# The top bits of the weights' low words: cut out by ScalarE from a byte, instead of by VectorE with a shift

## The chip, the cores and the metric

The kernel runs on one core of a Trainium2 chip. The metric is device time in microseconds (us) of one execution. TensorE multiplies matrices, VectorE and ScalarE work on tiles of 128 partitions, GpSimd does a few multiplications, and SyncE's queue (SP) issues nearly all DMAs. Each engine runs its own instructions in the order in which the program gives them, and waits on semaphores for the others.

## The reference

The queries, keys and values arrive as 32-bit floats, the weights as 64-bit floats. The computation is attention over 4 batches of 8 heads (576 positions, 64 wide), followed by two feed-forward layers on the 2304 x 512 result:

```
scores = q @ k^T / sqrt(64), masked: heads 0-3 a local window of 32,
         heads 4-7 every 32nd position (both causal)
x = softmax(scores) @ v                      # 2304 x 512
x = ((x @ w_a) * (x @ w_b)) @ w_out          # 512 -> 1536 -> 512
h = x @ w_in
out = (h * sigmoid(h)) @ w_out2              # 512 -> 2048 -> 512
```

## The kernel before

The 64-bit weights are read as pairs of 32-bit integers, low word first. The kernel puts each pair together to one 32-bit float with integer operations, and then splits that float into a rounded part and a remainder, with which each product takes three matmul passes.

The weights are cut into 68 pieces of 128 x 512: 36 for the first layer (kinds a, b and o) and 32 for the second (i and p). The work of the two layers is a list of 340 blocks; each block uses one piece on one group of up to 512 tokens and has 12 matmuls. The order of phases is: first layer of group 0, first layer of group 1, second layer of group 0, second layer of group 1, then the other groups. In the first round over the pieces a block also merges the piece that a later block needs: `conv_at` says that block p merges piece p + 3 up to block 32, and from block 34 on one piece in every 1.8 blocks. Six pieces (`EARLY`) are merged still earlier, during the attention of batch 0, with `early=True`. The attention of the other three batches is spread over the blocks as background work.

A merge has these steps, each an instruction on a 128 x 512 tile:

- `rebase_w` (L570, ScalarE): scales the high word as a float into the tile e.
- `merge_w` step 0 (L582, VectorE): takes the top three bits of the low word into a new tile "raw".
- step 1 (L585, VectorE): takes the sign bit of the high word and joins it to "raw".
- step 2 (L590, VectorE): shifts e left by three and joins "raw" to it. Now raw holds the float.
- `keep_w` (L601, SP): writes raw to DRAM, from where later groups load it again (`load_raw`, L560).
- `split_w` (L608 on ScalarE, L609 on VectorE): rounded part and remainder of a piece, into the tile w that the matmuls read.

In a block the order of the steps is given by a string of letters, 0, 1, 2 for the merge steps, B for the rebase, K for keep, Y for split, O for the attention output, X for its softmax, W for loads:

```
STEPS = ("RM0BK1O2YXWN", "0O1B2MKWYRXN")
```

The first string holds for blocks 0 to 35, the second for the others. Ahead of these steps the block puts its matmuls into TensorE's queue, with the background's loads, matmuls and copies of turned probabilities (L461, L467) before them; behind the steps it puts the evacuation of its PSUM tile: a copy (L818) for kind a, a product (L821) and a split (L626, L627) for kind b, a tanh (L825), a product (L827) and a split for kind i. So an engine meets the steps of block p only after the evacuation of block p-1.

The tiles "raw" come from a pool of five buffers, which merged pieces share with pieces that are loaded again; the words from another of five, the tiles e from one of two. A new tile waits until the readers of the former tile in its buffer, DMAs among them, are done.

The functions that the change touches:

Of the kernel before, what the change touches and what calls it, by code (L numbers as in the profile page):

```python
# [10 lines left out]
F32R = mybir.dt.float32r  # L11
BF16 = mybir.dt.bfloat16
I32 = mybir.dt.int32
AF = mybir.ActivationFunctionType
ALU = mybir.AluOpType
AX = mybir.AxisListType
# [71 lines left out]
def attention_gated_mlp_silu_mlp(  # L88
# [15 lines left out]
    nc = tc.nc  # L104
# [84 lines left out]
    class Batch:  # L189
# [213 lines left out]
        def softmax(self, u):  # L403
# [10 lines left out]
            for s in range(segs):  # L414
                nc.scalar.activation(  # L415
                    out=place[s],
                    in_=src[:, s],
                    func=AF.Exp,
                    bias=st["nm"][:, s:s + 1],
# [114 lines left out]
    words, raw, split, kept, rebased, loaded = {}, {}, {}, {}, {}, set()  # L534

    def load_words(c):
# [4 lines left out]
        w = {"a": w_a, "b": w_b, "o": w_out, "i": w_in2, "p": w_out2}[kind]  # L541
        words[c] = t = kpool.tile([P, 2 * DM], I32, tag="words", name="words")
        if kind in "op":
# [19 lines left out]
    def rebase_w(c, early=False):  # L563
# [4 lines left out]
        high = words[c].rearrange("p (n two) -> p n two", two=2)[:, :, 1]  # L568
        rebased[c] = e = epool.tile([P, DM], I32, tag="e", name="e")
        nc.scalar.activation(out=e.bitcast(F32), in_=high.bitcast(F32), func=AF.Copy, scale=REBASE)  # L570

    made = {}

    def merge_w(c, step, early=False):
        if c is None or (c < EARLY and not early):
            return
        pair = words[c].rearrange("p (n two) -> p n two", two=2)
        low, high = pair[:, :, 0], pair[:, :, 1]
        if step == 0:
            made[c] = rpool.tile([P, DM], F32, tag="raw", name="raw")  # L580
            z = made[c].bitcast(I32)
            nc.vector.tensor_single_scalar(out=z, in_=low, scalar=29, op=ALU.logical_shift_right)  # L582
        elif step == 1:
            z = made[c].bitcast(I32)
            nc.vector.scalar_tensor_tensor(  # L585
                out=z, in0=high, scalar=SIGN, in1=z, op0=ALU.bitwise_and, op1=ALU.bitwise_or
            )
        else:
            z = made[c].bitcast(I32)
            nc.vector.scalar_tensor_tensor(  # L590
                out=z, in0=rebased.pop(c), scalar=3, in1=z, op0=ALU.logical_shift_left, op1=ALU.bitwise_or
            )
            del words[c]
            if c < NA:
                raw[c] = made[c]
# [76 lines left out]
    def block(p):  # L672


        background(p, "load", "tensor", "turned")
        w = split.pop(p)
        yield w
        c = conv_at.get(p)
        for step in STEPS[p >= NA]:
            if step == "K":  # L680
                keep_w(conv_at.get(p - 1))
            elif step == "B":
                rebase_w(c)
            elif step in "012":
                merge_w(c, int(step))
            elif step == "Y":
                split_w(p + AHEAD_SPLIT)
                if p >= NB - NP:
                    split_w(p + AHEAD_SPLIT + 1)
            elif step == "W":  # L690
                load_words(conv_at.get(p + AHEAD_WORDS - AHEAD_MERGE))
                load_raw(p + (7 if p < last_conv + 2 else 9))
            else:
                background(p, {"M": "mask", "O": "store", "X": "softmax", "N": "normalise", "R": "prepare"}[step])
        yield None


    with tc.manual_schedule():
# [51 lines left out]
        for s in range(-1, max(nu + LV, max(PART), max(CONV) + 1) + 1):  # L750
# [7 lines left out]
            for step in ORDER:  # L758
# [4 lines left out]
                elif step in "SVTXLGNOU":  # L763
                    f, d = {
                        "S": (batch.scores, 0), "L": (batch.largest, 0), "X": (batch.softmax, 1),
                        "G": (batch.guard, 1), "N": (batch.normalise, 1), "T": (batch.turn, LT),
                        "U": (batch.turned, LT), "V": (batch.values, LV), "O": (batch.store, LV),
                    }[step]
                    stage(f, d)
                elif step == "K":  # L770
                    keep_warm(WARM1.get(s, 0))
                elif step == "A" and s in PART:
                    i = PART[s]
                    partial[i] = acc_tile(i)
                    up(partial[i], split[i], x_tile(0), G, (0, 1))
                elif step == "Q":
                    for i in TQ.get(s, ()):
                        batch.transpose_qk(1, i)
                elif step == "R":
                    for u in PREP.get(s, ()):  # L780
                        batch.prepare(u)
                elif step in "012" and now is not None:
                    merge_w(now, int(step), True)
                elif step == "B" and now is not None:
                    rebase_w(now, True)
                elif step == "Y" and last is not None and last < EARLY:
                    keep_w(last)
                    split_w(last)
                elif step == "W":
                    startup_loads(LOADS.get(s, ""))  # L790
        batch = after
        every(batch.load_vl())
        p = 0
        ys = {}
        for ph, g in PHASES:
# [7 lines left out]
            for kind, j in half[ph]:  # L803
# [4 lines left out]
                if kind in "abi":  # L808
# [14 lines left out]
                    else:  # L823
                        th = tpool.tile([P, G], F32, tag="a", name="th")
                        nc.scalar.activation(out=th[:, :T], in_=ps[:, :T], func=AF.Tanh, scale=0.5)  # L825
                        g2 = tpool.tile([P, G], F32, tag="h32", name="g2")
                        nc.vector.scalar_tensor_tensor(  # L827
                            out=g2[:, :T], in0=th[:, :T], scalar=1.0, in1=ps[:, :T], op0=ALU.add, op1=ALU.mult
                        )
                        hs[j] = split_act(g2, T)  # L830
                elif kind == "o":
# [10 lines left out]
                    if j == N1 - 1:  # L842
                        ys[g] = y = xpool.tile([P, 2, CC, G], F32R, tag="x%d" % HOMES["y"][g], name="y")
                        for d in range(CC):
                            nc.scalar.copy(out=y[:, 0, d, :T], in_=accs[d][:, :T])
                            nc.vector.tensor_tensor(
                                out=y[:, 1, d, :T],
                                in0=accs[d][:, :T],
                                in1=y[:, 0, d, :T].bitcast(F32),
                                op=ALU.subtract,  # L850
# [78 lines left out]
```

## Time and profile before

| | |
|---|---|
| time, median of 3 runs | 982.34 us (982.01 to 983.16) |
| profiled execution | 982.31 us |
| its span, first to last instruction | 980.5 us |
| mean granted TensorE clock | 0.993 of full speed |
| busy TensorE / VectorE / ScalarE / GpSimd | 958.2 / 611.4 / 474.5 / 40.3 us |

The span is the time from the first to the last instruction of the profiled execution; the time around it, 1.81 us, belongs to the device time. Durations below come from this execution. A busy engine isn't an engine at its peak: matmuls are pipelined and their ends are modelled, so that 12 matmuls that follow each other at their pace are listed with 2.88 us but start 2.72 us apart from the next twelve. In a timeline, a number in brackets is the time that the engine was idle just before the instruction, and the instruction that ended it.

### The profile page before, as it was taken

Reading aid. Unit: us, or ns where it says so; the run is one execution under the profiler, and the core shown is the slowest. Engines: PE = TensorE matmul, PEld = TensorE weight load, DVE = VectorE, ACT = ScalarE, POOL = GpSimd, SP = SyncE. Lnnn points to the kernel's source line nnn. Section 1 sums busy time; section 2 is a strip of 40 time slices with the busy share of each in tenths; the row PEclk is TensorE's granted clock in tenths of the full one; section 3 lists DMA queues with packets and bytes.
Section 4 is the critical chain, followed back from the end, with each engine's and each line's share of the span. In section 5 each row is a group of like instructions: output and inputs, shape, how many; then the busy total and the mean of one; then the engine's idle time right before and its main releaser. Section 6 shows DMA issues by size and latency. Waiting matters only on the chain.

```text
span 980.5 us, 16035 instructions
## 1 busy us (share of the span) xinstructions
PE 958.2 (98%) x5740; PEld 781.7 (80%) x5746; DVE 611.4 (62%) x1160; ACT 474.5 (48%) x1142; POOL 40.3 (4%) x66
## 2 busy tenths in 40 slices
PE   9989999999998999999999999999999999999998
PEld 5767677788777778888887888888888888889997
DVE  4788888878777864554644456554544454456675
ACT  3655556544555544544344445444333353445564
POOL 2100000000000000100000000000000000000000
PEclk9999999999999999999999999999999999999999
DMA  8899868898876763543364333323433323246551
GB/s 169 195 245 288 253 190 240 254 307 249 252 233 201 234 186 106 152 111 98 99 182 101 100 89 87 87 76 94 143 97 96 98 86 100 94 137 199 181 183 65
DMA packets 177647, 155.79 MB, mean 159 GB/s; under 512 B 102048, under 2 KB 125088, under 8 KB 177568
## 3 DMA queue, kind: packets, MB, share of 16 engines
q1 hardware_dynamic: 174198, 149.73, 53.2%
q0 software_dynamic: 1280, 4.20, 1.2%
q10 hardware_dynamic: 2090, 0.84, 0.4%
q8 instruction: 45, 0.74, 0.3%
q14 instruction: 34, 0.28, 0.1%
HBM read 132.19 MB, written 22.54 MB: 158 GB/s over the span
## 4 chain that ended last, share of the span: by engine, by line
PE 81%; DVE 9%; DMA 4%; issue 2%; ACT 2%; SPq 1%; DVEq 0%; ACTq 0%
PE ring L616 43%; PE acc L863 19%; PE acc L835 12%; PE att L378 2%; DVE raw L585 2%; DVE w L609 2%; PE att L489 1%; DVE raw L582 1%; DVE raw L590 1%; DMA vl<-in_v_dram 1%; DMA keptb<-raw 1%; DMA pair<-in_k_dram 1%; ACT h L626 1%; DMA kepta<-raw 1%; PE att L449 1%
## 5 line engine op out<-in xcount | busy, mean ns | idle before, releaser
L616 PE MATMUL ring<-x,w 128*128 128x512 f32 (+1 forms) x1392 | 303.0, 372 | 1.1 <-DVE w L609 1.1
L609 DVE TENSOR_TENSOR w<-raw,w 128x512 fp32r<-128x512 f32 x340 | 226.5, 685 | 87.3 <-ACT w L608 82.2
L616 PEld LDWEIGHTS ring<-x,w 128*128 128x128 f32 x1392 | 242.6, 190 | 46.3 <-DVE w L609 2.3
L616 PE MATMUL ring<-y,w 128*128 128x512 f32 (+1 forms) x960 | 211.4, 370 | 2.3 <-DVE w L609 2.2
L863 PE MATMUL acc<-w,h 128*128 128x512 f32 x864 | 212.1, 394 | 1.3 <-DVE w L609 1.3
L608 ACT CAST w<-raw 128x512 fp32r<-128x512 f32 x340 | 201.4, 618 | 10.0 <-DVE raw L590 9.6
L616 PEld LDWEIGHTS ring<-y,w 128*128 128x128 f32 x960 | 167.8, 188 | 34.3 <-DVE w L609 3.6
L863 PEld LDWEIGHTS acc<-w,h 128*128 128x128 f32 x864 | 160.5, 189 | 36.0 <-DVE w L609 2.2
L835 PE MATMUL acc<-h,w 128*128 128x512 f32 (+1 forms) x720 | 161.5, 374 | 0.3 <-DVE h L821 0.3
L835 PEld LDWEIGHTS acc<-h,w 128*128 128x128 f32 x720 | 126.0, 190 | 23.9 <-DVE h L821 0.7
L827 DVE SCALAR_TENSOR_TENSOR g<-th,ring 128x512 f32<-128x512 f32 (+1 forms) x80 | 50.5, 632 | 89.7 <-ACT th L825 88.5
L825 ACT ACTIVATE th<-ring 128x512 f32<-128x512 f32 (+1 forms) x80 | 44.3, 553 | 111.9 <-PE ring L616 111.6
L626 ACT CAST h<-h 128x512 fp32r<-128x512 f32 (+1 forms) x60 | 34.7, 578 | 121.4 <-DVE h L821 121.4
L627 DVE TENSOR_TENSOR h<-g,h 128x512 fp32r<-128x512 f32 (+1 forms) x80 | 51.1, 639 | 51.5 <-ACT h L626 51.5
L818 ACT COPY a<-ring 128x512 f32<-128x512 f32 (+1 forms) x58 | 31.4, 542 | 105.2 <-PE ring L616 105.2
L626 ACT CAST h<-g 128x512 fp32r<-128x512 f32 (+1 forms) x80 | 46.2, 578 | 70.1 <-DVE g L827 70.1
L627 DVE TENSOR_TENSOR h<-h,h 128x512 fp32r<-128x512 f32 (+1 forms) x60 | 38.3, 639 | 38.6 <-ACT h L626 38.6
L415 ACT ACTIVATE prs<-sm,nm 128x54 f32<-128x54 f32 (+1 forms) x120 | 39.8, 333 | 35.5 <-DVE nm L401 35.5
L440 POOL TENSOR_TENSOR prs<-prs,rs 128x256 f32<-128x256 f32 (+3 forms) x36 | 27.5, 764 | 587.6 <-ACT w L608 290.4
L590 DVE SCALAR_TENSOR_TENSOR raw<-e,raw 128x512 int32<-128x512 int32 x68 | 46.9, 689 | 6.3 <-ACT e L570 0.9
L821 DVE TENSOR_TENSOR h<-ring,a 128x512 f32<-128x512 f32 (+1 forms) x58 | 36.5, 629 | 22.1 <-PE ring L616 22.0
L585 DVE SCALAR_TENSOR_TENSOR raw<-words,raw 128x512 int32<-128x512 int32 x68 | 48.4, 712 | 2.3
(111 smaller groups left out, 513.3 us busy)
## 6 DMA issues: line engine op xcount, KB each, us to landing
raw<-kepti SPq DMA_DIRECT2D x80, 256.0 KB
raw<-keptp SPq DMA_DIRECT2D x80, 256.0 KB
words<-in_moe_w_out_dram SPq DMA_DIRECT2D x28, 512.0 KB
raw<-kepta SPq DMA_DIRECT2D x48, 256.0 KB
raw<-keptb SPq DMA_DIRECT2D x48, 256.0 KB
raw<-kepto SPq DMA_DIRECT2D x48, 256.0 KB
words<-in_moe_w_in_dram SPq DMA_DIRECT2D x16, 512.0 KB
words<-in_moe_w_a_dram SPq DMA_DIRECT2D x12, 512.0 KB
```

Source lines behind the costliest of these rows:

```text
L415: nc.scalar.activation(out=place[s], in_=src[:, s], func=AF.Exp, bias=st["nm"][:, s:s + 1], scale=1.0, accum_out=su[:, s:s + 1],)
L585: nc.vector.scalar_tensor_tensor(out=z, in0=high, scalar=SIGN, in1=z, op0=ALU.bitwise_and, op1=ALU.bitwise_or)
L590: nc.vector.scalar_tensor_tensor(out=z, in0=rebased.pop(c), scalar=3, in1=z, op0=ALU.logical_shift_left, op1=ALU.bitwise_or)
L608: nc.scalar.copy(out=o[:, 0], in_=t)
L609: nc.vector.tensor_tensor(out=o[:, 1], in0=t, in1=o[:, 0].bitcast(F32), op=ALU.subtract)
L616: nc.tensor.matmul(ps[:, :T], lhsT=w[:, wi, c * P:(c + 1) * P], rhs=x[:, xi, c, :T], start=(c == 0 and wi == 0 and xi == 0), stop=(c == CC ...
L626: nc.scalar.copy(out=o[:, 0, :T], in_=t32[:, :T])
L627: nc.vector.tensor_tensor(out=o[:, 1, :T], in0=t32[:, :T], in1=o[:, 0, :T].bitcast(F32), op=ALU.subtract)
L825: nc.scalar.activation(out=th[:, :T], in_=ps[:, :T], func=AF.Tanh, scale=0.5)
L827: nc.vector.scalar_tensor_tensor(out=g2[:, :T], in0=th[:, :T], scalar=1.0, in1=ps[:, :T], op0=ALU.add, op1=ALU.mult)
L835: nc.tensor.matmul(accs[d][:, :T], lhsT=w[:, wi, d * P:(d + 1) * P], rhs=h[:, xi, :T], start=(j == 0 and wi == 0 and xi == 0), stop=(j == ...
L863: nc.tensor.matmul(accs[t][:, :DM], lhsT=h[:, xi, t * P:(t + 1) * P], rhs=wj[:, wi, :], start=(jj == 0 and wi == 0 and xi == 0), stop=(jj ...
```

## The change

Step 0 of the merge, for all but the six early pieces, becomes an instruction of ScalarE. It reads the words as bytes, takes of each pair the fourth byte (the top byte of the low word), multiplies it by 1/32 and subtracts 31/64; written as the nearest integer, this is the byte divided by 32 and rounded down, which are the top three bits. Its place in the program is that of the instruction before: in ScalarE's queue it stands ahead of the rebase of the same piece.

```diff
+U8 = mybir.dt.uint8
 ...
         if step == 0:
             made[c] = rpool.tile([P, DM], F32, tag="raw", name="raw")
             z = made[c].bitcast(I32)
-            nc.vector.tensor_single_scalar(out=z, in_=low, scalar=29, op=ALU.logical_shift_right)
+            if early:
+                nc.vector.tensor_single_scalar(out=z, in_=low, scalar=29, op=ALU.logical_shift_right)
+            else:
+                top = words[c].bitcast(U8).rearrange("p (n eight) -> p n eight", eight=8)[:, :, 3]
+                nc.scalar.activation(out=z, in_=top, func=AF.Copy, scale=1.0 / 32, bias=-31.0 / 64)
```

## Rows read from the trace of the kernel before

**Rows 1.** Page: busy us of each engine; chain that ended last, by engine, by line

```profile
PE 958.2 (98%) x5740; PEld 781.7 (80%) x5746; DVE 611.4 (62%) x1160; ACT 474.5 (48%) x1142; POOL 40.3 (4%) x66
...
PE 81%; DVE 9%; DMA 4%; issue 2%; ACT 2%; SPq 1%; DVEq 0%; ACTq 0%
PE ring L616 43%; PE acc L863 19%; PE acc L835 12%; PE att L378 2%; DVE raw L585 2%; DVE w L609 2%; PE att L489 1%; DVE raw L582 1%; DVE raw L590 1%; DMA vl<-in_v_dram 1%; DMA keptb<-raw 1%; DMA pair<-in_k_dram 1%; ACT h L626 1%; DMA kepta<-raw 1%; PE att L449 1%
```

**Rows 2.** Stretches: length, busy us of each engine; clock, DMA share, GB/s

```profile
100.00:125.00 25.00, 21.32 (x119) 16.25 (x119) 22.09 (x49) 14.55 (x32) 0.40 (x1) 0.93 0.80 241
500.00:600.00 100.00, 100.00 (x599) 80.42 (x599) 49.46 (x94) 43.96 (x105) 3.69 (x5) 1.00 0.38 101
```

**Rows 3.** Waits of TensorE: line <- what it waited for, us in total, times, longest

```profile
PE att L489 <- ACT ptl L461: 5.8, 4, 2.7
PE ring L616 <- DVE w L609: 3.3, 4, 1.5
PE att L378 <- DVE x L512: 2.7, 2, 2.4
...
PE acc L863 <- DVE w L609: 1.3, 2, 0.8
```

**Rows 4.** Groups by line: tile shapes, count, busy us, mean ns, idle before

```profile
L608 ACT CAST w<-raw 128x512 fp32r<-128x512 f32 x340 | 201.4, 618 | 10.0 <-DVE raw L590 9.6
...
L585 DVE SCALAR_TENSOR_TENSOR raw<-words,raw 128x512 int32<-128x512 int32 x68 | 48.4, 712 | 2.3
...
L570 ACT ACTIVATE e<-words 128x512 f32<-128x512 f32 x68 | 45.9, 675 | 1.5 <-DMA words<-in_moe_w_b_dram 1.3
...
L582 DVE TENSOR_SCALAR raw<-words 128x512 int32<-128x512 int32 x68 | 29.1, 428 | 1.7 <-DMA keptb<-raw 1.6
```

**Rows 5.** Timeline of TensorE: start us, length us, instructions, idle before

```profile
101.50 0.69 PE L489 MATMUL att<-ptl,vl 128*64 128x64 f32 x16 [2.38 <-ACT ptl L461]
102.11 4.60 PE L616 MATMUL ring<-x,w 128*128 128x512 f32 x12
...
110.15 2.88 PE L835 MATMUL acc<-h,w 128*128 128x512 f32 x12
...
125.19 1.58 PE L378 MATMUL att<-kT,qs 64*64 64x54 f32 x18 [2.37 <-DVE x L512]
126.69 3.67 PE L616 MATMUL ring<-x,w 128*128 128x512 f32 x9
...
187.03 8.00 PE L616 MATMUL ring<-x,w 128*128 128x512 f32 x34 [0.86 <-DVE w L609]
...
292.04 2.59 PE L616 MATMUL ring<-y,w 128*128 128x512 f32 x10 [1.54 <-DVE w L609]
...
300.54 1.12 PE L489 MATMUL att<-ptl,vl 128*64 128x64 f32 x16 [2.68 <-ACT ptl L461]
...
324.05 2.56 PE L616 MATMUL ring<-y,w 128*128 128x512 f32 x10 [0.64 <-DVE w L609]
```

**Rows 6.** Timelines of VectorE (DVE) and ScalarE (ACT), 80 to 125 us

```profile
80.93 0.43 DVE L582 TENSOR_SCALAR raw<-words 128x512 int32<-128x512 int32 x1 [1.64 <-DMA keptb<-raw]
...
99.34 0.68 DVE L821 TENSOR_TENSOR h<-ring,a 128x512 f32<-128x512 f32 x1
...
102.01 0.39 DVE L582 TENSOR_SCALAR raw<-words 128x512 int32<-128x512 int32 x1
...
124.85 0.28 DVE L512 TENSOR_TENSOR x<-att,x 128x128 fp32r<-128x128 f32 x1
...
84.48 0.68 ACT L570 ACTIVATE e<-words 128x512 f32<-128x512 f32 x1 [1.32 <-DMA words<-in_moe_w_b_dram]
...
100.70 0.74 ACT L461 COPY ptl<-att 64x256 f32<-64x256 f32 x2
101.47 0.69 ACT L570 ACTIVATE e<-words 128x512 f32<-128x512 f32 x1
```

## The prediction, made before the kernel was run

> **What bounds the kernel now.** I read the page first: busy times, then the chain that ended last. TensorE is busy for 958.2 of 980.5 us and carries 81% of the chain, so most of the time is matmuls that the change doesn't touch; VectorE has 9% of the chain, and the three merge lines and the split (L582, L585, L590, L609) are its largest entries [rows 1]. The reader is to see that the share of L582 in the chain, 1%, is small but not nothing.
>
> An average hides where this is, so next come the stretches. From 100 to 125 us, where one weight piece is merged in each block, VectorE is busy 22.09 of 25 us, and what is left is mostly the pauses between dependent instructions; TensorE is busy for only 21.32. From 500 to 600 us, with no merge, TensorE is busy all of the time and VectorE half [rows 2]. ScalarE has 14.55 of 25 us in the first stretch. All L582 instructions lie before 351 us, so nothing after that can gain.
>
> Third, what TensorE waited for. Four rows name a late VectorE or ScalarE: 5.8, 3.3, 2.7 and 1.3 us, 13.1 together [rows 3]. This is the ceiling of a direct gain, plus what the clock adds: after the two long pauses of [rows 5] the next matmuls run slower (12 in 4.60 us, and 9 in 3.67, where 12 take 2.88), and the mean granted clock of that stretch is 0.93 against 1.00 later [rows 2, 5], so part of it ran at 1.2 instead of 2.4 GHz. That is some 1.7 and 1.5 us more (3.67 - 9/12 x 2.88 = 1.5).
>
> **The change part by part.** It removes 62 of the 68 L582 instructions from VectorE (the six early pieces keep theirs): 62 x 0.428 = 26.5 us of its time [rows 4]. It adds 62 ACTIVATEs to ScalarE. None in the trace reads bytes and writes integers. The nearest is L570, which reads one 32-bit word in every 8 bytes, as the new one reads one byte in every 8: 0.675 us; the cast L608, without a stride, takes 0.618; the far end would be the longest single-tile VectorE pass over such data, 0.712 [rows 4], and 1.0 if the byte input costs extra, which no row shows. I take 0.675, so 41.9 us more on ScalarE. No DMA, no matmul and no PSUM slot is added.
>
> What moves with it are the waits: for the loaded words and for a free "raw" buffer. They stand now in VectorE's queue and will stand in ScalarE's, ahead of the rebase, the attention output, the split and the softmax of the block. And L585 gets a wait it doesn't have now, for ScalarE; behind it on VectorE are L590, L609 and the next evacuation, for which TensorE waits in [rows 3].
>
> Does ScalarE come early enough? The new instruction stands directly ahead of the rebase L570, and L570 was idle for only 1.5 us over all its 68 instances [rows 4]: ScalarE walks straight into it, and stands still after it, where it needs VectorE. So the start of L570 is where the new one will start. In all ten blocks from 88 to 124 us L570 starts ahead of L582; the narrowest pair is 101.47 against 102.01 [rows 6]. The result is then ready at 101.47 + 0.675 + 0.05 for the semaphore = 102.2, where L585 without L582 could start at 102.0: a loss of 0.2 at the worst, none at most others. The saving per block on VectorE is thus the 0.43 of L582.
>
> *First place, 80 to 126 us.* Here VectorE runs almost without a gap, and both long TensorE pauses end on it: that at 101.50 through the probability copy (ptl) at 100.70, which ScalarE reaches only after a cast for which it waited on VectorE's L821 at 99.34; and that at 125.19 through the attention remainder (x) of 124.85 [rows 5, 6]. Twelve L582 lie between 80.9 and 124 us. Ten of them are met with VectorE late: 10 x 0.43 = 4.3. Two (the first is the 80.93 one, which had waited 1.64 for a DMA; the second comes at 84.49 with the words that L570 waited for until 84.48 [rows 6]) are released by DMA, and there the path becomes 0.675 + 0.05 instead of 0.43: 2 x 0.3 = 0.6 lost. The narrow pair costs 0.2, and the split behind it, which ScalarE reaches 0.57 later, about 0.1. So 4.3 - 0.6 - 0.3 = 3.4: TensorE restarts at 121.8 instead of 125.19. What the first pause gives back, its 1.7 us of low clock included, is swallowed by this second one. Whether the low clock after the second goes is unclear: 0 to 1.5, and I take 0, since the pause shrinks but the work around it is still small attention matmuls.
>
> *Second place, 150 to 250 us.* The rest of the L378 row (2.7 - 2.37 = 0.35) goes, since VectorE is then 3 us earlier. The 0.86 at 187.03 [rows 5] follows two L582 that stand between VectorE's last wait on TensorE and this split: 0.86, of which 0.2 is lost because the new instruction then stands behind the four y casts: 0.65. The two small waits in the L489 row (5.8 - 2.38 - 2.68 = 0.75) lie behind at least one L582 each: 0.75. Sum 1.75.
>
> *Third place, 285 to 355 us.* 1.54 at 292.04 and 2.68 at 300.54 come from one run of VectorE with two L582: 0.85 of the 4.22. The 0.64 at 324.05 lies behind two: it goes. The 1.3 of the L863 row [rows 3], at about 345 and 353, lies behind five: it goes. Sum 2.8.
>
> *Against it:* at 82.0 us an attention remainder frees a PSUM tile for TensorE's scores just in time; the DMA-released block ahead of it now has the new instruction in ScalarE's queue before the x cast: 0.4. Bounds of this term are 0 and 1.5.
>
> Sum: 3.4 + 1.75 + 2.8 - 0.4 = 7.55. The profiled execution took 982.31 (980.5 of span and 1.81 around it), 0.03 under the median of 982.34. So 982.31 - 7.5 = 974.8. If all terms are at their good ends (low clock gone, 0.43 everywhere, nothing against): 982.3 - 7.95 - 1.5 - 0.9 = 972; if freed time also lets the first place start earlier, down to 968, since 13.1 + 3.2 is all there is (966).
>
> **Rivals.**
> *A: the loads are the bound in the first place.* From 100 to 125 us the DMA engines are 0.80 busy [rows 2], and two of the twelve merges there were released by a DMA. If the words or the buffers' write-backs are late for all of them, VectorE only waits longer, and only the second and third places give: 982.3 - 4.5 + 0.6 = 978.4. Against it: ten of twelve didn't wait.
>
> *B: ScalarE becomes the bound and it gets slower.* Mechanism: the new instruction holds ScalarE's queue for a DMA or a buffer that VectorE's own order freed before; rebase, x cast, split and softmax stand behind it, and TensorE behind these. Place: the first, up to block 32. Price per block 0.675 + 0.05 - 0.43 = 0.3, and 30 merges lie there: 9 us; the later places then also give about 2 instead of 4.5: 982.3 + 9 - 2 = 989. It decides from where more than some fifteen of the thirty are released late (15 x 0.3 = 4.5, the gain of the others). For it: two such blocks are seen, and in block pairs without an evacuation ScalarE must now wait for VectorE's L609 to free a buffer. Against it: that lead in all ten blocks, of which [rows 6] shows the narrowest, and 10.4 us of spare ScalarE time in 25 [rows 2]. The Trainium skill ("ScalarE: Activation LUTs", Rules for kernel authors) speaks for this rival: it says that multiplies and adds belong on VectorE, not ScalarE. The rows agree on the price (0.675 against 0.428), not on which engine is late; by that rule the time would be this rival's.
>
> *C: no difference.* The gain in the first place is lost to A, and ScalarE's later splits cancel the rest (4.5 - 0.6 - 3): 981.4. Or the new instruction takes 1.0 us, which uses up the shorter leads.
>
> **How the numbers follow.** Forecast (970 to 977.5, named as 974.8): 0.58. A: 0.15. C: 0.12. B: 0.15. A measurement of this kernel can tell 0.2%, 2 us, from no change. Faster by over 0.2% is the forecast and A: 0.73; within it C: 0.12; slower B: 0.15. The range from 968 to 984 holds the forecast, A and C, and leaves out most of B and a gain beyond all named waits.
>
> **What would show it.** Right: VectorE some 26 us less busy, ScalarE some 42 more; the new line 0.62 to 0.71 us; the waits of TensorE at about 125, 187, 324 and 345 us gone or smaller, that at 300 still there; L585 with little idle time for the new line. Wrong: idle time of VectorE before L585 of more than 5 us, put down to ScalarE; ScalarE idle before the new line for DMA or L609; new TensorE waits on splits or x; or the same waits of TensorE with a DMA as their end.

## The result, and the profile after

The changed kernel took 976.81 us in the median of 9 runs (972.15 to 980.58), the kernel before in the same rounds 983.91 (982.01 to 989.81). The ratio is 0.991 with a 95% interval of 0.9883 to 0.9938: 6 to 11.5 us faster. The profiled execution took 977.48 us, with a span of 975.7.

Page after: busy us of each engine; the chain by engine and line (lines have moved: the new instruction is L589, the former L585, L590, L608, L609 are L592, L597, L615, L616).

```profile
PE 959.9 (98%) x5746; PEld 782.9 (80%) x5746; DVE 587.4 (60%) x1098; ACT 508.0 (52%) x1204; POOL 41.5 (4%) x66
...
PE 85%; DVE 7%; ACT 2%; DMA 2%; issue 2%; SPq 1%; DVEq 0%; ACTq 0%
```

Against [rows 1], VectorE is 24.0 us less busy and ScalarE 33.5 more (its 41.5 of new work, of which each instruction overlaps the next by some 0.1 us), and TensorE's share of the chain rose from 81% to 85%.

Groups by line after: shapes, count, busy us, mean ns, idle before:

```profile
L592 DVE SCALAR_TENSOR_TENSOR raw<-words,raw 128x512 int32<-128x512 int32 x68 | 47.3, 695 | 13.8 <-ACT raw L589 13.2
...
L571 ACT ACTIVATE e<-words 128x512 f32<-128x512 f32 x68 | 45.3, 667 | 0.0
L589 ACT ACTIVATE raw<-words 128x512 int32<-128x512 uint8 x62 | 41.5, 670 | 4.2 <-DMA keptb<-raw 2.3 <-DMA words<-in_moe_w_b_dram 1.1 <-DVE w L616 0.6
```

The new instruction takes 0.670 us, as the rebase beside it; the byte input and the integer output cost nothing extra. The waits for DMA that stood at L570 and L582 [rows 4] stand at L589 now, and VectorE waits 13.2 us for it, of which more below.

Waits of TensorE after, against [rows 3]:

```profile
PE att L490 <- ACT ptl L462: 3.1, 2, 2.2
PE att L379 <- DVE x L513: 2.9, 3, 1.4
PE att L379 <- DVE kT L230: 1.6, 2, 1.2
PE ring L623 <- DVE w L616: 1.3, 2, 1.1
```

The four rows that named a late VectorE or ScalarE fell from 13.1 to 7.3 us; the one of L863 is gone. Timeline of TensorE after, against [rows 5]:

```profile
85.19 0.67 PE L379 MATMUL att<-kT,qT 64*32 64x64 f32 x24 [1.44 <-DVE x L513]
85.80 4.61 PE L623 MATMUL ring<-x,w 128*128 128x512 f32 x12
...
103.56 0.69 PE L490 MATMUL att<-ptl,vl 128*64 128x64 f32 x16
...
108.65 0.42 PE L379 MATMUL att<-kT,qT 64*32 64x64 f32 x14 [1.22 <-DVE x L513]
...
124.61 1.54 PE L379 MATMUL att<-kT,qs 64*64 64x54 f32 x18 [0.24 <-DVE x L513]
126.08 4.62 PE L623 MATMUL ring<-x,w 128*128 128x512 f32 x12
...
185.77 8.00 PE L623 MATMUL ring<-x,w 128*128 128x512 f32 x34 [0.23 <-DVE w L616]
...
281.91 0.70 PE L379 MATMUL att<-kT,qT 64*32 64x64 f32 x32
...
289.81 2.60 PE L623 MATMUL ring<-y,w 128*128 128x512 f32 x10 [1.08 <-DVE w L616]
...
297.86 1.12 PE L490 MATMUL att<-ptl,vl 128*64 128x64 f32 x16 [2.20 <-ACT ptl L462]
298.91 4.01 PE L870 MATMUL acc<-w,h 128*128 128x512 f32 x12
...
347.73 0.45 PE L490 MATMUL att<-ptl,vl 128*64 128x64 f32 x8 [0.89 <-ACT ptl L462]
```

The pause of 2.38 us before the attention values is gone (103.56 has none), that of 2.37 is 0.24, and 0.86 is 0.23. New against this execution of the kernel before are 1.44 at 85.19, with a low clock behind it (12 matmuls in 4.61 instead of 3.01 in the same block before, at a granted clock of 0.63), and 1.22 at 108.65; the latter isn't new against every execution (experiment 9).

**Two starts.** The profile after is late from the beginning. The first matmul of the background's scores is a mark that all kernels here share and that lies ahead of nearly all that the change touches. Before and after, that matmul:

```profile
58.03 0.30 PE L378 MATMUL att<-kT,qT 64*32 64x64 f32 x2 [1.22 <-DVE kT L229]
```

```profile
61.36 0.30 PE L379 MATMUL att<-kT,qT 64*32 64x64 f32 x2 [1.22 <-DVE kT L230]
```

and the stretch ahead of it (length; busy us of TensorE, its loads, VectorE, ScalarE, GpSimd; granted clock, DMA share, GB/s), before and after:

```profile
25.00:50.00 25.00, 24.63 (x293) 18.68 (x292) 18.33 (x52) 17.24 (x76) 4.82 (x6) 1.00 0.86 200
```

```profile
25.00:50.00 25.00, 24.89 (x230) 18.18 (x229) 14.29 (x40) 14.48 (x68) 4.62 (x6) 0.73 0.88 216
```

After, the clock was granted at 1.2 GHz for part of that stretch (mean 0.73), and the mark came 3.33 us later. This is not the change: in a second profile of the kernel before, the clock there is 0.86 and the mark at 59.49 us, and seven of the thirteen profiles in all had less than 1.00. So I measure profiles from the mark to the end of the span: 980.5 - 58.03 = 922.5 before, 975.7 - 61.36 = 914.3 after, 8.1 us less.

From the mark the gain accrues so. Where the matmuls start behind the pause at 125: 126.69 - 58.03 = 68.66 before [rows 5], 126.08 - 61.36 = 64.72 after, 3.9 gained. At the scores of 281.91 (283.69 before): 5.1. At 298.91 (301.59 before): 6.0. At the end: 8.1. This is one execution of each kernel; experiment 9 has a second pair, with nearly the same total and other parts.

### The profile page after: what moved, and what is told of

Same layout as the page of the kernel before. It is cut to its first block, busy times and chain, and to the rows that moved or that the text cites. A ratio compares the mean times of both kernels' runs of the same rounds, so it can differ in the third digit from the quotient of the medians.

```text
span 975.7 us, 16041 instructions
## 1 busy us (share of the span) xinstructions
PE 959.9 (98%) x5746; PEld 782.9 (80%) x5746; DVE 587.4 (60%) x1098; ACT 508.0 (52%) x1204; POOL 41.5 (4%) x66
## 4 chain that ended last, share of the span: by engine, by line
PE 85%; DVE 7%; ACT 2%; DMA 2%; issue 2%; SPq 1%; DVEq 0%; ACTq 0%
PE ring L623 45%; PE acc L870 19%; PE acc L842 13%; PE att L379 2%; PE att L490 2%; DVE raw L592 1%; DVE w L616 1%; DVE raw L597 1%; PE att L450 1%; DMA pair<-in_k_dram 1%; PE acc L715 1%; DMA kepta<-raw 1%; ACT raw L589 1%; PE acc L367 1%; PE ring L367 1%
## 5 line engine op out<-in xcount | busy, mean ns | idle before, releaser
L616 DVE TENSOR_TENSOR w<-raw,w 128x512 fp32r<-128x512 f32 x340 | 226.7, 685 | 88.0 <-ACT w L615 83.2
L615 ACT CAST w<-raw 128x512 fp32r<-128x512 f32 x340 | 201.3, 618 | 3.2 <-DVE raw L597 2.9
L592 DVE SCALAR_TENSOR_TENSOR raw<-words,raw 128x512 int32<-128x512 int32 x68 | 47.3, 695 | 13.8 <-ACT raw L589 13.2
L597 DVE SCALAR_TENSOR_TENSOR raw<-e,raw 128x512 int32<-128x512 int32 x68 | 47.3, 696 | 6.0 <-ACT w L615 0.5
```

What stands on the lines that cost most here:

```text
L592: nc.vector.scalar_tensor_tensor(out=z, in0=high, scalar=SIGN, in1=z, op0=ALU.bitwise_and, op1=ALU.bitwise_or)
L597: nc.vector.scalar_tensor_tensor(out=z, in0=rebased.pop(c), scalar=3, in1=z, op0=ALU.logical_shift_left, op1=ALU.bitwise_or)
L615: nc.scalar.copy(out=o[:, 0], in_=t)
L616: nc.vector.tensor_tensor(out=o[:, 1], in0=t, in1=o[:, 0].bitcast(F32), op=ALU.subtract)
```

## The experiments

Theory: VectorE's queue was late for TensorE in three places, and ScalarE, though it is given more work than VectorE loses, had room ahead of it. Rivals: ScalarE's queue as the new bound, the loads as the bound in the first place, and a gain that is all in one stretch. Each ratio is to the kernel before in the same rounds on the same chip; medians of different rows are not always from one chip, so compare ratios.

| kernel | median us | ratio, 95% interval | mark us | mark to end us |
|---|---|---|---|---|
| before / run again | 983.91 / 985.11 | - / 1.001 (0.999 to 1.0031) | 58.03 / 59.49 | 922.5 / 921.7 |
| changed / run again | 976.81 / 973.48 | 0.991 / 0.9888 (0.986 to 0.9916) | 61.36 / 61.53 | 914.3 / 914.5 |
| 1 extra on ScalarE | 984.79 | 0.9996 (0.9978 to 1.0014) | 61.61 | 925.9 |
| 2 no top bits | 972.95 | 0.9865 (0.9842 to 0.9889) | 57.48 | 909.1 |
| 3 first layer only | 980.52 | 0.9943 (0.9922 to 0.9964) | 57.29 | 916.4 |
| 4 second layer only | 979.44 | 0.9941 (0.9919 to 0.9964) | 57.49 | 917.1 |
| 5 write-backs elsewhere | 972.84 | 0.9875 (0.985 to 0.9899) | 61.66 | 912.4 |
| 6 rebase first | 980.98 | 0.9955 (0.9936 to 0.9973) | 57.76 | 919.6 |
| 7 a block earlier | 972.02 | 0.9883 (0.9848 to 0.9918) | 57.50 | 912.4 |
| 8 both (5 and 7) | 974.62 | 0.9901 (0.9879 to 0.9924) | 61.62 | 911.2 |
| 9 more warm matmuls | 976.26 | 0.9908 (0.9888 to 0.9928) | 65.83 | 913.4 |

The column from the mark is one execution each, and low clock after a pause comes and goes in it: the two profiles of the changed kernel agree within 0.2 us, the two of the kernel before within 0.8.

**1. The price alone: the new instruction on ScalarE, the shift kept on VectorE.**

```diff
+        if not early:
+            top = words[c].bitcast(U8).rearrange("p (n eight) -> p n eight", eight=8)[:, :, 3]
+            nc.scalar.activation(out=e, in_=top, func=AF.Copy, scale=1.0 / 32, bias=-31.0 / 64)
         nc.scalar.activation(out=e.bitcast(F32), in_=high.bitcast(F32), func=AF.Copy, scale=REBASE)
```

> This kernel keeps the shift on VectorE and gives ScalarE the new instruction as well, 62 times, into the tile e just before the rebase overwrites it; so ScalarE pays the whole price of the change (41.5 us) and VectorE gets nothing. Theory (VectorE's queue was late, ScalarE had room): within 2 us of the kernel before, ratio 0.998 to 1.003, and TensorE's waits the same as before. Rival (ScalarE becomes a bound once it has the new work): 5 us or more slower, ratio 1.005 or above, with new waits of TensorE on splits or attention copies.

Measured: 0.9996, so 41.7 us more work on ScalarE costs between -2.2 and +1.4 us. ScalarE had the room for the time. What this kernel doesn't have is the wait for a free "raw" buffer in ScalarE's queue, and VectorE's wait for the result: the new instruction writes into e here. Experiments 5 and 6 are about these two. The waits of its profile (an execution with the low clock at its start, and the longest of twelve; L620 and L613 are the former L616 and L609):

```profile
PE att L490 <- ACT ptl L462: 6.5, 4, 2.7
PE ring L620 <- DVE w L613: 4.8, 5, 1.5
PE att L379 <- DVE x L513: 4.1, 4, 2.4
```

They are those of [rows 3], with 3.6 us more in these three rows, as the rival had it; but the ratio is over all runs and shows no loss, and this one profile can't settle why.

**2. The relief alone: nobody takes the top bits.**

```diff
-            else:
-                top = ...
-                nc.scalar.activation(out=z, in_=top, ...)
 ...
-                out=z, in0=high, scalar=SIGN, in1=z, op0=ALU.bitwise_and, op1=ALU.bitwise_or
+                out=z, in0=high, scalar=SIGN, in1=z if early else high,
+                op0=ALU.bitwise_and, op1=ALU.bitwise_or if early else ALU.bitwise_and
```

> This kernel leaves the top bits of the low words of the 62 pieces out altogether: neither engine computes them, and L592 joins the sign with the high word instead (same shape, same count). It shows what the change would give if the new work on ScalarE were free. Theory: ScalarE's part costs little, only where VectorE now waits for it (13.2 us of idle time before L592 in all, of which few microseconds reach TensorE): 2 to 4 us below the changed kernel, ratio to the kernel before 0.985 to 0.989. Rival (the new work on ScalarE eats half of the gain): 8 us or more below the changed kernel, ratio 0.983 or less. If the loads set the pace, no faster than the changed kernel: 0.990 to 0.993.

Measured: 0.9865; from the mark 5.2 us less than the changed kernel, by the two ratios 2.3 to 4.4 us less, though the intervals overlap. So the relief of VectorE is worth some 13 us. ScalarE's part, the waits that moved into its queue included, costs a sixth to two fifths of that if the difference is taken as it stands; that it costs nothing while VectorE is late (experiment 1) and something once it is not is a reading, not shown apart. Its profile shows where: in the changed kernel 1.44 of pause at 85.19 with the low clock behind it, and a low clock again at 126.08; without the top bits, 0.74 and none. These two low clocks, some 1.6 us each, are 3.2 of the 5.2. On the other side it pauses for 1.40 at 98.23, where the changed kernel doesn't (the first line is the same scores):

```profile
80.21 0.67 PE L379 MATMUL att<-kT,qT 64*32 64x64 f32 x24 [0.74 <-DVE x L513]
...
98.23 0.69 PE L490 MATMUL att<-ptl,vl 128*64 128x64 f32 x16 [1.40 <-ACT ptl L462]
...
118.72 1.54 PE L379 MATMUL att<-kT,qs 64*64 64x54 f32 x18 [0.24 <-DVE x L513]
```

**3 and 4. Half of the pieces each.**

```diff
-            if early:
+            if early or c >= NA:     # 3: first layer only
+            if early or c < NA:      # 4: second layer only
```

> Only the pieces of the first layer (30 of the 62) are cut by ScalarE; the 32 of the second layer keep the shift on VectorE. From the two traces, the changed kernel gained 3.9 us between the first background scores and the long pause at 125, and 0.65 at the change of groups at 186; the rest, 3.6, came later. Theory: about 4.6 us of the 8.2 gained from that first mark on, ratio 0.994 to 0.997, and the waits at 290 to 355 as before. Rival (the gain is all in the late stretch, and the first is paid back by the loads): no faster than before, 0.998 to 1.002.

> Only the pieces of the second layer (32 of the 62, merged from block 34 on) are cut by ScalarE. Theory: the late part of the gain alone, some 3.6 us (0.5 at 248, 0.9 at 290 to 300, 2.2 from 320 to 355), ratio 0.995 to 0.998; the two long pauses at 101 and 125 us stay as in the kernel before. Rival (all of the gain comes from the first stretch): within 0.1% of the kernel before.

Measured: 0.9943 and 0.9941. Each half gives a gain of its own; neither rival holds, and the loads don't set the pace of the first stretch. The second half gave 5.8 us by its ratio (3.5 to 8.0), 5.4 from the mark, more than the expected 3.6. Together the halves are 11.4 us by the ratios and 11.5 from the mark. The whole is 8.9 and, run again, 11.0 by its ratios, so the times show no surplus of the halves; from the mark the whole is 8.1 and 7.2. In the profile of the first half the clock stays at 1.00 from 75 to 150 us, where the changed kernel has 0.93 twice, so a part of what the single profiles differ by is low clock that comes or not. The rest stays open: why the second half alone gives some 2 us more than its share of the whole in the first pair of profiles wasn't tried. The long pauses stayed where expected in kernel 4:

```profile
100.91 0.69 PE L490 MATMUL att<-ptl,vl 128*64 128x64 f32 x16 [2.39 <-ACT ptl L462]
101.52 4.61 PE L623 MATMUL ring<-x,w 128*128 128x512 f32 x12
...
124.61 1.54 PE L379 MATMUL att<-kT,qs 64*64 64x54 f32 x18 [2.37 <-DVE x L513]
```

**5. The late buffer: four write-backs from another queue.**

```diff
-            nc.sync.dma_start(out=t, in_=made.pop(c))
+            queue = nc.gpsimd if EARLY <= c < EARLY + 4 else nc.sync
+            queue.dma_start(out=t, in_=made.pop(c))
```

> The changed kernel, with the write-backs of the first four merged pieces (6 to 9) issued from GpSimd's queue instead of SyncE's. In the changed kernel ScalarE waits 2.29 us at 83.19 for the write-back of piece 6, which SyncE issues only after a row of attention loads; TensorE then pauses for 1.44 us and its next 12 matmuls take 4.61 instead of 2.88. Theory (a late buffer, now on ScalarE, is the price of the change in the first stretch): that wait of ScalarE goes, and 1.4 to 3.2 us of device time with it, ratio 0.987 to 0.991. Rival (the loads of the words set the pace there): the wait for the words, 1.08 at 86.76, grows instead and the time stays within 1 us of the changed kernel.

In the changed kernel, ScalarE and VectorE at that place:

```profile
83.19 0.68 ACT L589 ACTIVATE raw<-words 128x512 int32<-128x512 uint8 x1 [2.29 <-DMA keptb<-raw]
...
86.76 0.67 ACT L589 ACTIVATE raw<-words 128x512 int32<-128x512 uint8 x1 [1.08 <-DMA words<-in_moe_w_b_dram]
```

and in this kernel:

```profile
81.08 0.68 ACT L589 ACTIVATE raw<-words 128x512 int32<-128x512 uint8 x1
...
86.52 0.66 ACT L589 ACTIVATE raw<-words 128x512 int32<-128x512 uint8 x1 [1.64 <-DMA words<-in_moe_w_b_dram]
```

The wait for the buffer is gone and the pause at 85 with it; half a microsecond of it came back as wait for the words, TensorE then paused 1.82 us at 103.05, and ScalarE waited 2.9 us for another write-back at 207, which it didn't in the changed kernel. The time is 0.9875 against 0.9888 for the changed kernel in the same rounds, 2 us from the mark: on the expected side, but the intervals overlap, so the gain in time is not shown.

**6. The other order on ScalarE: rebase first.**

```diff
-STEPS = ("RM0BK1O2YXWN", "0O1B2MKWYRXN")
+STEPS = ("RMB0K1O2YXWN", "BO012MKWYRXN")
```

> The changed kernel with ScalarE's two instructions of a merge in the other order: first the rebase, then the top bits. VectorE's L592 needs the top bits first, so it comes 0.57 us later wherever ScalarE is only just ahead. Theory (the gain rests on ScalarE being ahead of VectorE, with L592 waiting at 12 places now): L592's idle time for ScalarE grows from 13.2 to over 18 us, and the time by 1 to 4 us, ratio 0.992 to 0.996. Rival (the wait of L592 is never on TensorE's path): as the changed kernel within 0.5 us.

Waits of VectorE for the new instruction in this kernel:

```profile
DVE raw L592 <- ACT raw L589: 29.0, 36, 3.4
```

From 13.2 us at 12 places to 29.0 at 36, and the ratio 0.9955 against 0.9888 for the changed kernel in the same rounds, with intervals that don't overlap: half of the gain or more is lost by some 0.57 us of lateness on ScalarE (an estimate: the 0.667 of the rebase less the overlap of 0.1). This is the clearest sign that the gain hangs on ScalarE's lead over VectorE, and that the lead is thin.

**7. A block earlier on ScalarE.**

```diff
             elif step in "012":
-                merge_w(c, int(step))
+                if step != "0":
+                    merge_w(c, int(step))
 ...
+        merge_w(conv_at.get(p + 1), 0)
         yield None
```

> The changed kernel with the top bits taken one block earlier on ScalarE: the instruction for the next block's piece stands at the end of this block's steps, ahead of the evacuation, where ScalarE mostly waits for TensorE or VectorE. Theory (what is left of the price is L592 waiting for ScalarE behind an evacuation): L592's 13.2 us of idle time falls under 6, and the time goes 1 to 4 us below the changed kernel, towards the 0.9865 of the kernel without top bits. Rival (a buffer is needed a block earlier and none is free): ScalarE's own waits for DMA or L616 grow by over 5 us, and the time is that of the changed kernel or above.

Waits of ScalarE in this kernel:

```profile
ACT raw L589 <- DVE w L616: 8.1, 8, 1.8
ACT raw L589 <- DMA words<-in_moe_w_b_dram: 3.2, 1, 3.2
ACT raw L589 <- DMA keptb<-raw: 3.0, 1, 3.0
```

L592's wait fell to 6.9 us, less than expected, and the rival's price is there: ScalarE now waits 8.1 us for VectorE's splits to free a buffer (0.6 in the changed kernel) and 10 for DMAs (3.4). VectorE has a wait instead that it didn't have: its L597 (the third step) waits 4.5 us for the rebase, so its waits for ScalarE in a merge are 11.4 us in place of 13.2. The ratio, 0.9883, is that of the changed kernel (0.9888).

**8. Both edits of 5 and 7.**

> The changed kernel with both edits: the top bits taken one block earlier on ScalarE, and the write-backs of pieces 6 to 9 from GpSimd's queue. Theory (they mend different waits: one the instructions behind an evacuation, the other the late buffer near 83 us, which with the first edit alone still holds ScalarE for 3.0 us and TensorE for 1.4 to 1.7 twice): 2 to 4 us below the changed kernel, ratio 0.983 to 0.988, and no wait of ScalarE for a write-back before 130 us. Rival (each frees only what the other frees too, and the words' loads are next): as the changed kernel with one of the edits, 0.9875 to 0.989.

0.9901, with the interval up to 0.9924: no gain over the changed kernel. The wait for a write-back near 83 us is gone as expected, that for the words is 4.0, and L597 waits 4.9 us for the rebase. From the mark it is the best but for kernel 2 (911.2); the times don't bear it out. A version that beats the changed kernel was not found.

**9. The start: the kernel before again, the changed one again, and more matmuls on constants.**

```diff
-WARM1 = {-1: 2, 0: 4, 2: 2, 3: 7, 4: 1, 5: 3, 7: 4, 9: 2, 12: 2}
+WARM1 = {-1: 2, 0: 4, 2: 2, 3: 7, 4: 3, 5: 5, 6: 2, 7: 4, 9: 2, 12: 2}
```

> The kernel before as it is, for a second look at its start and at the spread of its times (981.7 to 989.8 us in the runs so far). Theory (the chip lowers the clock between 25 and 45 us in some executions of any of these kernels): ratio 0.998 to 1.002; if the profile has less than 1.00 of granted clock in 25 to 50 us, its first background scores come near 61 us and its total near 986; if it has 1.00, near 57.5 to 58 and 982. Rival (only the changed kernels do this): always 1.00 and 58 us here.

> The changed kernel as it is, beside the others on one chip, for comparison and for a second look at its start. In its first profile the stretch from 25 to 50 us ran at a mean granted clock of 0.73, and the first background scores came at 61.4 us; in the kernel before, 1.00 and 58.0. Theory (that start is the chip's choice and not the change's, since the instructions up to there are the same): the ratio is 0.989 to 0.994 again, and a profile with 1.00 in that stretch, if it comes, has the scores at 57.3 to 58.1. Rival (the change itself brings on the slow start): again 0.73 there.

> The changed kernel with six more of the matmuls on constants that stand between the attention's small matmuls, two each at three steps between 22 and 35 us (some 1.4 us of TensorE time). In five of the profiles so far the granted clock is 0.73 (four) or 0.86 (one) on the mean of 25 to 50 us and the first background scores come at 61.4 to 61.7 (0.73) or 59.5 us; in six others it is 0.93 or 1.00. Theory (the low clock there follows from small matmuls, and is most of the spread of the times): a clock of 1.00 in 25 to 50 us, scores at 58.5 to 59.5 us, a spread under 5 us and a median of 971 to 974. Rival (the clock falls there whatever TensorE does): 0.73 again in part of the runs, a spread of 8 us, and the median about 1 us above the changed kernel's.

The stretch from 25 to 50 us in the kernel before, run again, and in the kernel with more such matmuls:

```profile
25.00:50.00 25.00, 24.62 (x258) 18.35 (x259) 16.20 (x46) 15.21 (x70) 4.80 (x6) 0.86 0.96 237
```

```profile
25.00:50.00 25.00, 25.00 (x196) 16.96 (x193) 11.54 (x35) 12.68 (x63) 4.19 (x6) 0.63 0.90 217
```

The kernel before has the low clock there too, so the change doesn't bring it on. The changed kernel, run again, had 0.73 once more, but five kernels with its instructions or most of them (2, 3, 4, 6, 7) had 1.00. My theory of the cause fell: with more matmuls on constants the clock was at its lowest, 0.63, the mark at 65.83 and the spread 7.3 us. What lowers it stays open. (Where that expectation counts six profiles at 0.93 or 1.00, there were seven.)

The second profiles also test the account by places. In the kernel before, run again, TensorE did this:

```profile
101.65 0.69 PE L489 MATMUL att<-ptl,vl 128*64 128x64 f32 x16 [2.39 <-ACT ptl L461]
102.27 3.02 PE L616 MATMUL ring<-x,w 128*128 128x512 f32 x12
...
107.08 0.42 PE L378 MATMUL att<-kT,qT 64*32 64x64 f32 x14 [1.57 <-DVE x L512]
107.44 4.60 PE L616 MATMUL ring<-x,w 128*128 128x512 f32 x12
...
125.61 1.54 PE L378 MATMUL att<-kT,qs 64*64 64x54 f32 x18 [1.22 <-DVE x L512]
127.08 3.06 PE L616 MATMUL ring<-x,w 128*128 128x512 f32 x12
...
300.68 5.47 PE L863 MATMUL acc<-w,h 128*128 128x512 f32 x12
```

The pause at 101 is the same as in [rows 5], but no low clock follows it. A pause of 1.57 stands at 107 (none in [rows 5]), that at 125 is half as long and has no low clock behind it, and the low clock behind the pause at 300 is longer (3.96 us for 12 matmuls in the first profile). The changed kernel did nearly the same in both its profiles. Of the second pair, the gain from the mark is 2.8 us behind the pause at 125 (67.59 - 64.78), 2.7 at the scores of 281.91, 3.6 at 298.91 and 7.2 at the end, where the first pair had 3.9, 5.1, 6.0 and 8.1. So the total holds within a microsecond, and how it divides among the places doesn't.

## Why the prediction was right

The forecast was 974.8 and a gain of 7.5 us; measured were 976.81 and 6 to 11.5 us, 8.1 from the mark. By its steps:

- *What bounds it.* Right: experiment 1 shows that ScalarE's time is not it, 2 that VectorE's is, 3 and 4 that it is in both stretches.
- *First place, 3.4 less 0.4.* 3.9 came in the first pair of profiles and 2.8 in the second, but not from the terms that I summed; that the sum is so near is in part luck. The term that failed is "against it": I gave 0.4, with bounds of 0 and 1.5, for the block at 82 us that a DMA releases, and it became a pause of 1.44 with a low clock behind it. From matmul to matmul that is 3.4 us in the first pair and 2.9 in the second; in kernel 5, without the wait for the write-back, both are gone.

  What made up for it in the first pair: the pauses at 101 and 125 shrank by 4.5 of 4.75 and the low clock behind the first went (1.6), where I had let the second pause swallow the first; and 2.4 came ahead of 80 us, for which I had nothing (1.6 of it a low clock: 12 matmuls in 4.58 at 74.40 before, in 3.00 at 76.85 after; the rest are waits for loads and for VectorE). Against it, 1.22 at 108.65. 4.5 + 1.6 + 2.4 - 1.2 - 3.4 = 3.9.

  In the second pair the kernel before has no low clock near 74 and has a pause at 107, so these two terms are not shown to be the change's. The pause at 101 is: 2.38 and 2.39 before, none after in either. For the low clock behind the second pause I took 0: the changed kernel has it in both profiles (4.62 for 12 matmuls), the kernel before in one (4.37; 3.06 in the other).
- *Second place, 1.75, of which 0.33 belongs behind 350 us.* 1.2 came in the first pair (5.1 - 3.9) and nothing in the second (2.7 - 2.8), where the low clock behind the pause at 125 is the changed kernel's alone. The 0.86 at 187 lost 0.63 in both, as worked out.
- *Third place, 2.8 and those 0.33.* 3.0 came in the first pair (8.1 - 5.1): 1.54 became 1.08 and 2.68 became 2.20 (0.94 for 0.85), 0.64 and the 1.3 went whole, but the 0.33 at 351 grew to 0.89. These rows make 2.3; the other 0.7 is not explained. In the second pair it is 4.6 (7.2 - 2.7), 1.5 of it the longer low clock at 300 in the kernel before.
- *The rivals.* A (loads): some of it is there, the words' wait of 1.1 to 1.6 at 86 us, but the first half alone gains 0.0036 or more. B (ScalarE): excluded by 1. The rule of the Trainium skill ("ScalarE: Activation LUTs", Rules for kernel authors) that puts multiplies and adds on VectorE agrees with the price, 0.670 for the multiply and add on ScalarE against 0.428 for the shift on VectorE [rows 4], and was the wrong guide here. C: excluded by the interval.
- *ScalarE's lead.* The price of 0.675 was right (0.670); the 1.0 that I allowed for bytes stood on no row. In the ten blocks from 88 to 124 us the lead held: L592 doesn't wait for ScalarE there. But the sign that I had named for a wrong prediction did come: L592 waits 13.2 us for ScalarE in all, not under 5. The step that failed is the one from ten blocks to all. Four of the twelve waits, 3.3 us in all, lie ahead of these blocks (74 to 88 us); of the other eight, the four over 1 us lie where TensorE's timeline after has no pause. That VectorE there only waits early for what it would have waited for later is my reading; no run tests it. Two of them, in the timeline of VectorE after:

```profile
216.75 0.69 DVE L592 SCALAR_TENSOR_TENSOR raw<-words,raw 128x512 int32<-128x512 int32 x1 [1.95 <-ACT raw L589]
...
269.27 0.69 DVE L592 SCALAR_TENSOR_TENSOR raw<-words,raw 128x512 int32<-128x512 int32 x1 [2.71 <-ACT raw L589]
```

The same page of the Trainium skill ("ScalarE: Activation LUTs", What ACT_TABLE_LOAD costs) prices an ACTIVATE with immediate scale and bias at 186 ns and 0.833 ns per element, by which an estimate for 512 elements is 613 ns; the cast L615 (618) agrees, and the two that read every eighth byte or every second word (670 and 667) take 57 and 54 ns more than that.

## What to carry to other kernels

In this kernel, which engine should do a step was decided by which queue is late where TensorE waits, not by who does it faster: 41.5 us of ScalarE's time bought 26.5 of VectorE's, at a gain, because ScalarE stood idle ahead of VectorE. Compare the start times of the two engines' neighbouring instructions, block by block, to see whether there is a lead; and where a DMA releases the moved step, count the clock that may fall behind a pause (some 1.6 us for 12 matmuls here), not the pause alone. When single profiles are compared, fix a mark behind the start first: here the start alone moved by up to 4 us between executions of the same instructions. And profile both kernels twice before dividing a gain among places: here 8.1 and 7.2 us agreed, 3.9 and 2.8 in the first place didn't.

## What the runs showed that I had not expected

- A granted clock below full speed between 25 and 50 us in some executions, from 1.00 down to 0.73 on the mean with the same instructions, worth 3.3 to 4 us at the mark (57.3 to 61.6), with TensorE busy for 24.6 to 24.9 of the 25 us either way. That it is a large part of the spread of 8 us between runs of one kernel is an estimate from these marks. It hid 3.3 us of the gain in the comparison of the two first profiles (4.8 us instead of 8.1).
- A pause of 0.24 us was followed by the low clock (4.62 us for 12 matmuls at 126.08) in both profiles of the changed kernel, and by none in kernels 2 and 3 (3.06 us), at the same place behind the same small matmuls; one of 1.22 there was followed by none in the kernel before, run again. So the length of the pause alone doesn't tell what the clock will do.
- ScalarE reads bytes at a stride of eight and writes 32-bit integers in 0.670 us for 128 x 512, as it reads and writes 32-bit floats at that stride.
